# Interleaving two chunks' products and the weight product W in a fused attention and expert kernel

## Chip, cores and metric

One core of one Trainium2 chip (trn2). The metric is the device time of one execution in microseconds (us); the median of several runs is given. Engines: TensorE (PE, and PEld for its weight loads), VectorE (DVE), ScalarE (ACT), GpSimd (POOL), SyncE (SP, which issues all DMAs here).

## What is computed

Inputs: q, k, v of 4 batches x 8 heads x 576 x 64, float32; float64 weights w1, w2 (512 x 1024), w3 (1024 x 1024), w_out (1024 x 512); four experts of 512 x 1024 and 1024 x 512, float32.

```
q_s = softmax(q, over the head's 64); k_s = softmax(k, over the sequence)
x   = q_s @ (k_s.T @ v)                  per batch and head, then 2304 x 512
a, b = x @ w1, x @ w2
y   = ((a * b) @ w3) @ w_out
out = sum over experts e of p[e] * (relu(y @ e1[e]) @ e2[e]),  p = probs / sum
```

## The kernel before, in words

The tokens are cut into chunks of 512 (four, and one of 256); chunk c takes its x from the batches that hold its tokens. Every float32 product is made as three matmuls of a hi and a lo part (mm3, lines 106 to 110).

**Conversion.** w1, w2, w3 and w_out come as float64. Two 512 KB pieces make a pair (load_to, line 410). ScalarE takes the absolute value of the high words (line 123), VectorE runs four passes (lines 127 to 138), then split makes hi on ScalarE (line 102) and lo on VectorE (line 103). There are 20 pairs; the list `jobs` (384 to 386) gives their order: eight pairs of w1 and w2 slices, then pieces of w_out ("o") and of w3 ("w"). `AHEAD` loads four pairs ahead.

**Stages.** The work is written in slots, a hand-made order. Slots 6 to 13 (AB0) are ab_step(0, f): for slice f of 128 columns, a = x w1 and b = x w2 of chunk 0, 24 matmuls of 512 columns, the copy of a (479) and the product a times b (480), kept in SBUF in `prods`. The converted weights are also saved to DRAM (save_w12, 443). Slots 14 to 21 (AB1) are ab_step(1, f) with weights read back (load_w12, 448), mixed with W's units 0 to 7; slots 22 to 29 (W1) are units 8 to 15. W = w3 @ w_out is made once, 16 units of 12 matmuls (unit, 683), each block ended by a correction (454). Slots 30 to 45 are y_step for chunks 0 and 1 (h from `prods` by h_step, 486; 12 matmuls each), y stored by y_out. From slot 46 (REST) ab, h and y of chunk 2, then of chunks 3 and 4; then the experts to the end.

**Attention** of batch b is put into slots by K_SLOT, Q_SLOT and X_SLOT: k_max, k_exp, k_v (245), q_exp (266 to 288), q_norm, q_turn (313), x_stage (326, 343). Its inputs are loaded two or three slots ahead. q of batch 1, half 1 is exponentiated by ScalarE row by row (274, ON_SCALAR).

**Cooking.** From the y phase on the experts' weights are combined and split once and saved to DRAM (cooking, save_e at 608), one step a slot in the y phase, four to eight a slice later.

**Order.** A planner puts the instructions of each engine, and the DMA issues of SP, in one fixed order, from the written order as priority and its own estimate of when each is ready; so steps can move ahead of their slot. `hold(key, inst)` tells it to put an instruction behind others; it adds no wait at run time. Engines and SP's queue work in their order. `gran` tiles (4 KB a partition; x, weights, wo, w3, W, products, h) share NG = 28 slots.

Of the kernel before, what the change touches and what calls it, by code (L numbers as in the profile page):

```python
# [31 lines left out]
AB0, AB1, W1, Y0, Y1, REST = 6, 14, 22, 30, 38, 46  # L32
# [3 lines left out]
K_SLOT = [[0, 0, 0, 0], [6, 7, 8, 9], [30, 32, 34, 36], [46, 47, 48, 50]]  # L36
Q_SLOT = [[2, 2], [6, 8], [30, 34], [46, 48]]
X_SLOT = [AB0, AB1, REST, REST + 8]
# [4 lines left out]
    ("k", 1, 0): 2, ("k", 1, 1): 3, ("k", 1, 2): 4, ("k", 1, 3): 5, ("q", 1, 0): 2, ("q", 1, 1): 4,  # L43
# [7 lines left out]
ON_SCALAR = {(1, 1)}  # L51
# [3 lines left out]
def linear_attention_moe_kernel(ctx: ExitStack, tc, q, k, v, w1, w2, w3, wo, dp, e1, e2, out):  # L55
# [15 lines left out]
    NG, NR = 28, 4  # L71
# [34 lines left out]
    def mm3(ps, w_hi, w_lo, r_hi, r_lo, first, last, shared=False):  # L106
        kw = {"skip_group_check": True} if shared else {}
        nc.tensor.matmul(out=ps, lhsT=w_hi, rhs=r_hi, start=first, stop=False, **kw)  # L108
        nc.tensor.matmul(out=ps, lhsT=w_hi, rhs=r_lo, start=False, stop=False, **kw)  # L109
        nc.tensor.matmul(out=ps, lhsT=w_lo, rhs=r_hi, start=False, stop=last, **kw)  # L110
# [34 lines left out]
    class Act:  # L145
# [20 lines left out]
    def load_k(b, hp):  # L166
        t = ap_.tile([P, 2, KR + 1, D], F32, tag="kr", name="kr", bufs=4)
        src = k[b, 2 * hp:2 * hp + 2]
        nc.sync.dma_start(
            out=t[:, :, 0:KR], in_=src[:, 0:KR * P].rearrange("h (p r) d -> p h r d", p=P)  # L170
        )
        nc.sync.dma_start(out=t[0:KX, :, KR], in_=src[:, KR * P:S].rearrange("h p d -> p h d"))
        kraw[b, hp] = t

    def load_v(b, hp):
        t = ap_.tile([P, 2, KR + 1, D + 1], F32, tag="vt", name="vt", bufs=4)
        nc.gpsimd.memset(t[..., D:D + 1], 1.0)
# [142 lines left out]
    def x_stage(b, hp):  # L320
# [10 lines left out]
        for u in range(2):  # L331
            ps, a = pss[u], HALF * u
            t0 = S * b + a
            while t0 < S * b + a + HALF:
                c = t0 // CH
                n = min(chunks[c][0] + chunks[c][1], S * b + a + HALF) - t0
                i, o = t0 - S * b - a, t0 - chunks[c][0]
                hi, lo = (xa.at(c, hp, s, o, o + n) for s in range(2))
                if b > 1:
                    split(hi, lo, ps[:, i:i + n])  # L340
                else:
                    nc.scalar.activation(out=hi, in_=ps[:, i:i + n], func=ACTF.Copy)
# [5 lines left out]
                t0 += n  # L348

# [10 lines left out]
    for b in range(B):  # L360
        for j in range(2):
            s = Q_SLOT[b][j]
            if b > 0:
                put(before, s - 2, load_q, b, j)
# [4 lines left out]
        for i, hp in enumerate(PAIRS):  # L369
            s = K_SLOT[b][i]  # L370
            if b > 0:
                put(before, s - 3, load_kv, b, hp)
# [3 lines left out]
            put(after, min(s + (4 if b > 1 else 3), X_SLOT[b] - 1), x_stage, b, hp)  # L376
# [7 lines left out]
    jobs = [(x, f) for f in range(NF) for x in ("a", "b")]  # L384
    for u, (x, kt) in enumerate(UNITS):
        jobs += ([("o", kt)] if x == 0 else []) + [("w", u)]
# [5 lines left out]
    def load_to(m):  # L392
        while done["load"] < min(m, len(jobs) // 2):
# [3 lines left out]
            for i in range(2):  # L397
# [12 lines left out]
                nc.sync.dma_start(out=dst, in_=src)  # L410
# [9 lines left out]
    def b_to(m):  # L420
        while done["b"] < min(m, len(jobs) // 2):
# [23 lines left out]
    def load_w12(c, f):  # L445
        for i in range(2):
            g = gran("wg")
            gate["dma"] = [nc.sync.dma_start(out=g.bitcast(F32), in_=w12d[f, i])]
            w12.setdefault((c, f), []).append(g)
# [10 lines left out]
    hg, yps, Wg, prods, ps_z = {}, {}, {}, {}, []  # L460

    def ab_step(c, f):
# [6 lines left out]
        for i in range(2):  # L469
            ps = bank(ps_y[i] if c == 0 and f % 2 else ps_w, "ab")  # L470
            for x, kt in enumerate(PAIRS):
                o = P * kt
                mm3(
                    ps[:, 0:n], gw[i][:, 0, o:o + P], gw[i][:, 1, o:o + P],
                    xa.at(c, kt, 0), xa.at(c, kt, 1), x == 0, x == KT - 1,
                )
# [3 lines left out]
        nc.vector.tensor_tensor(out=ah, in0=pss[1][:, 0:n], in1=ah, op=ALU.mult)  # L480


    def h_step(c, f):
        n = chunks[c][1]
        h = gran("h")
        lo = split(h[:, 0, 0:n], h[:, 1, 0:n], prods[c, f // 2][:, f % 2, 0:n])[1]
        if (c, f) == (0, 3):
            gate["cook"] = [lo]
# [4 lines left out]
    def y_step(c, f):  # L493
# [11 lines left out]
        for d in range(KT):  # L505
            o = P * d
            mm3(
                yps[c, d], Wg[f][:, 0, o:o + P], Wg[f][:, 1, o:o + P],
                h[:, 0, 0:n], h[:, 1, 0:n], f == 0 and not (pair and d % 2), f == NF - 1, pair,
            )  # L510
# [13 lines left out]
    def x_free(c):  # L524
        for kk in list(xa.t):
            if kk[0] == c:
# [79 lines left out]
    def save_e(kind, n, name, g):  # L606
        ewd[kind, n, name] = d = dr.tile([P, 2, 2, 256], F32, name=f"{kind}_{n}_{name}")
        nc.sync.dma_start(out=d, in_=g.bitcast(F32))
# [3 lines left out]

    def cooking(pool):
        raws_e, waiting = {}, []
# [5 lines left out]
        def part_of(kind, n):  # L620
            def part(name, src):
                def do():
                    g = pool.tile([P, 2, 2, 256], F32R, tag="o", name="eo", bufs=NOUT)
                    for i in split(g[:, 0], g[:, 1], src):
                        hold("cook", i)
# [6 lines left out]
        for i, (kind, n) in enumerate(COOKED):  # L632
            ask(i + 1)
            for do in cook(kind, n, raws_e.pop(i), part_of(kind, n)):
                do()
                while len(waiting) > 2:
                    save_e(*waiting.pop(0))
                yield
        while waiting:
            save_e(*waiting.pop(0))  # L640
# [82 lines left out]
    for f in range(NF):  # L723
        convert(f + 2)
        slot(AB0 + f, (ab_step, 0, f))
        if f > 1:
            save_w12(f - 2)
    x_free(0)
    save_w12(NF - 2)
    save_w12(NF - 1)  # L730
    load_w12(1, 0)
    load_w12(1, 1)
    for f in range(NF):
        if f + 2 < NF:
            load_w12(1, f + 2)
        convert(8 + f + 1)
        slot(AB1 + f, (ab_step, 1, f), *([(unit, f - 1)] if f > 0 else []))
    x_free(1)
    unit(NF - 1)
    steps = [(c, f) for c in range(2) for f in range(NF)]  # L740
    for f in range(NF):
        convert(17 + f // 2)
        slot(W1 + f, (unit, 8 + f))
        if f % 2:
            h_step(*steps[f // 2])
# [7 lines left out]
    def cook_some(k):  # L753
        for _ in range(k):
            next(cooks, None)

    for i, (c, f) in enumerate(steps):
# [307 lines left out]
```

## Time and profile before

| | us |
|---|---|
| median of 3 runs | 1161.68 (1160.33 to 1163.48) |
| profiled execution | 1162.17 |
| its span | 1160.4 |
| PE / DVE / ACT / POOL busy | 1127.0 / 868.4 / 534.7 / 46.8 |

The profile is one execution. The span runs from the first to the last instruction; what lies around it is 1.8 us. Matmuls are pipelined, so that a busy PE is not PE at its peak: the time from one matmul's start to the next tells the rate.

### The profile page before, as it was taken

The page shows a single profiled execution, that of the slowest core. Times are in us where ns is not written, and L with a number is a line of the kernel's source. Part 1 is how long each engine was busy: PE and PEld are TensorE (multiplying, and loading weights), DVE is VectorE, ACT ScalarE, POOL GpSimd, SP SyncE. Part 2 cuts the span into 40 slices and gives each one's busy share as a digit, 9 for nine tenths or more (in the row PEclk, how much of TensorE's full clock was granted, in tenths as well). Part 3 has the DMA queues.
Part 4 walks back from the last instruction along what each step waited for, and adds up shares of the span by engine and source line. Part 5 has one row for each costly group of instructions (what it writes and reads, how often), then busy time and mean ns, then how long its engine had stood idle before and what let it go on. Part 6 is the DMA issues. An engine that isn't in the chain of part 4 may idle for free.

```text
span 1160.4 us, 18707 instructions
## 1 busy us (share of the span) xinstructions
PE 1127.0 (97%) x7048; PEld 1050.2 (91%) x7048; DVE 868.4 (75%) x1428; ACT 534.7 (46%) x982; POOL 46.8 (4%) x70
## 2 busy tenths in 40 slices
PE   5889999999999999999999999999999999999997
PEld 4667888787888889999999999999999999999997
DVE  7898866766457414999989987777779877777777
ACT  4665535555445315555555544433336344433441
POOL 0012300103000000000000000000000000000000
PEclk9999999999999999999999999999999999999999
DMA  9999960599799746777877888777777797777773
GB/s 238 264 352 305 372 233 1 183 381 405 282 378 356 277 164 224 288 286 283 295 275 273 287 303 307 251 251 251 250 249 257 244 305 256 248 253 249 241 262 111
DMA packets 127418, 310.12 MB, mean 267 GB/s; under 512 B 31968, under 2 KB 52960, under 8 KB 127328
## 3 DMA queue, kind: packets, MB, share of 16 engines
q1 hardware_dynamic: 126848, 308.14, 76.9%
q8 instruction: 56, 0.92, 0.3%
q10 hardware_dynamic: 480, 0.79, 0.2%
q14 instruction: 34, 0.28, 0.1%
HBM read 232.33 MB, written 76.55 MB: 266 GB/s over the span
## 4 chain that ended last, share of the span: by engine, by line
PE 86%; DVE 6%; DMA 5%; SPq 2%; issue 1%; ACT 1%; DVEq 0%; ACTq 0%
PE hp L879 28%; PE op L953 26%; PE ab L110 5%; PE ab L108 5%; PE ab L109 5%; PE y L108 3%; PE y L110 2%; PE y L109 2%; DMA kr<-in_k_dram 2%; DVE acc L937 2%; PE kv L245 2%; PE W L108 1%; PE W L109 1%; PE W L110 1%; DVE h L103 1%; DVE blk L588 1%
## 5 line engine op out<-in xcount | busy, mean ns | idle before, releaser
L953 PE MATMUL op<-eg,h 128*128 128x256 f32 x3024 | 379.9, 280 | 0.5 <-DMA eg<-e_b 0.4
L879 PE MATMUL hp<-t,eg 128*128 128x384 f32 x2016 | 377.1, 336 | 1.1 <-DVE acc L937 0.9
L953 PEld LDWEIGHTS op<-eg,h 128*128 128x128 f32 x3024 | 373.4, 188 | 1.0 <-PE hp L879 0.7
L879 PEld LDWEIGHTS hp<-t,eg 128*128 128x128 f32 x2016 | 344.6, 188 | 3.3 <-DVE acc L937 2.1
L937 DVE SCALAR_TENSOR_TENSOR acc<-op,prob,acc 128x256 f32<-128x256 f32 (+1 forms) x396 | 197.2, 527 | 43.1 <-PE op L953 43.1
L102 ACT ACTIVATE h<-blk 128x768 fp32r<-128x768 f32 x168 | 138.0, 842 | 144.5 <-DVE blk L588 108.2
L103 DVE TENSOR_TENSOR h<-blk,h 128x768 fp32r<-128x768 f32 x168 | 157.2, 950 | 24.4 <-ACT h L102 24.3
L862 ACT ACTIVATE blk<-hp 128x384 f32<-128x384 f32 x192 | 90.7, 490 | 138.8 <-PE hp L879 137.1
L866 DVE TENSOR_TENSOR blk<-hp,blk 128x384 f32<-128x384 f32 x144 | 79.3, 556 | 66.8 <-PE hp L879 63.6
L108 PE MATMUL ab<-x,wg 128*128 128x512 f32 (+1 forms) x320 | 121.1, 381 | 3.4 <-ACT wg L102 2.7
L109 PE MATMUL ab<-x,wg 128*128 128x512 f32 (+1 forms) x320 | 119.3, 373 | 0.2 <-ACT x L347 0.2
L110 PE MATMUL ab<-x,wg 128*128 128x512 f32 (+1 forms) x320 | 119.3, 375 | 0.0
L868 ACT ACTIVATE blk<-blk 128x768 f32<-128x768 f32 x72 | 60.6, 845 | 73.6 <-DVE blk L866 72.0
L588 DVE TENSOR_TENSOR blk<-blk 128x768 f32<-128x768 f32 x96 | 91.4, 952 | 0.5
L108 PEld LDWEIGHTS ab<-x,wg 128*128 128x128 f32 x320 | 60.8, 191 | 14.6 <-ACT wg L102 3.5
L109 PEld LDWEIGHTS ab<-x,wg 128*128 128x128 f32 x320 | 61.0, 191 | 10.8 <-ACT x L347 0.8
L110 PEld LDWEIGHTS ab<-x,wg 128*128 128x128 f32 x320 | 61.0, 191 | 10.8 <-DVE wg L103 0.5
L480 DVE TENSOR_TENSOR ah<-ab,ah 128x512 f32<-128x512 f32 (+1 forms) x40 | 25.4, 635 | 51.1 <-PE ab L110 46.5
L103 DVE TENSOR_TENSOR eo<-e2r,eo 128x512 fp32r<-128x512 f32 x56 | 41.6, 744 | 19.1 <-ACT eo L102 18.7
L109 PE MATMUL y<-h,W 128*128 128x512 f32 x128 | 50.3, 395 | 0.0
L110 PE MATMUL y<-h,W 128*128 128x512 f32 x128 | 49.4, 392 | 0.0
L108 PE MATMUL y<-h,W 128*128 128x512 f32 x128 | 47.9, 404 | 0.0
(98 smaller groups left out, 1037.2 us busy)
## 6 DMA issues: line engine op xcount, KB each, us to landing
eg<-e_t SPq DMA_DIRECT2D x96, 512.0 KB, 4.5
eg<-e_b SPq DMA_DIRECT2D x72, 512.0 KB, 4.8
eg<-e_s SPq DMA_DIRECT2D x68, 512.0 KB, 4.4
eg<-e_a SPq DMA_DIRECT2D x51, 512.0 KB, 4.6
wg<-w SPq DMA_DIRECT2D x48, 512.0 KB, 8.4
f<-in_moe_w_dram SPq DMA_DIRECT2D x32, 512.0 KB, 6.5
e_t<-eo SPq DMA_DIRECT2D x32, 512.0 KB, 6.3
e_s<-eg SPq DMA_DIRECT2D x28, 512.0 KB, 4.8
```

Source lines behind the costliest of these rows:

```text
L102: i = nc.scalar.activation(out=hi, in_=src, func=ACTF.Copy)
L103: j = eng.tensor_tensor(out=lo, in0=src, in1=hi.bitcast(F32), op=ALU.subtract)
L108: nc.tensor.matmul(out=ps, lhsT=w_hi, rhs=r_hi, start=first, stop=False, **kw)
L109: nc.tensor.matmul(out=ps, lhsT=w_hi, rhs=r_lo, start=False, stop=False, **kw)
L110: nc.tensor.matmul(out=ps, lhsT=w_lo, rhs=r_hi, start=False, stop=last, **kw)
L588: return lambda: nc.vector.tensor_tensor(out=dst, in0=x, in1=y, op=op)
L862: nc.scalar.activation(out=block(name)[:, u], in_=src, func=func)
L866: nc.vector.tensor_tensor(out=x[:, u], in0=src, in1=x[:, u], op=ALU.add)
L868: nc.scalar.activation(out=x, in_=x, func=ACTF.Relu)
L879: nc.tensor.matmul(out=q, lhsT=w[:, sw, kt, P * u:P * u + P], rhs=t[b][:, kt, st], start=new and kt == 0 and i == 0, stop=kt == 1 and i == ...
L937: nc.vector.scalar_tensor_tensor(out=dst, in0=src, scalar=prob[:, T, e:e + 1], in1=dst, op0=ALU.mult, op1=ALU.add,)
L953: nc.tensor.matmul(out=q[:, c:c + DH], lhsT=g[:, sh, u, P * i:P * i + P], rhs=w[:, sw, u], start=new and u == 0 and j == 0, stop=u == 1 an ...
```

## The change

Chunk 1's ab_step follows chunk 0's three slices behind (LAG) and uses the same converted weights, so that the weights are not read back for it. The order of conversion is ab pairs 0 to 4, then w_out and w3 pieces between the others; W's units start at slice 4 (WLAG 4). The products of chunks 0 and 1 are stored to DRAM and read back for h (load_ah). Batch 1's attention moves to slots 3 to 8, and its second q goes to VectorE. The part of chunk 2 that comes from batch 1 (128 tokens) is kept in one `early` tile and copied later. Loads of batches 2 and 3 are held until pair 13 is converted, those of batch 3 and of w for chunks 2 and on also behind the last matmul written ("pace"); weight loads from pair 2 on are held behind batch 1's last q load. Cooking makes two steps a slot in the y phase, held by "pace". NG is 26, and y has two buffers of its own.

```diff
-AB0, AB1, W1, Y0, Y1, REST = 6, 14, 22, 30, 38, 46
+LAG, WLAG = 3, 4
+AB0 = 6
+W1 = AB0 + 8 + LAG
+Y0 = W1 + 5
+REST = Y0 + 16
-K_SLOT = [[0, 0, 0, 0], [6, 7, 8, 9], [30, 32, 34, 36], [46, 47, 48, 50]]
-Q_SLOT = [[2, 2], [6, 8], [30, 34], [46, 48]]
-X_SLOT = [AB0, AB1, REST, REST + 8]
+K_SLOT = [
+    [0, 0, 0, 0], [3, 4, 5, 5], [Y0 - 2, Y0 - 0, Y0 - -2, Y0 + 4], [REST, REST + 1, REST + 2, REST + 4],
+]
+Q_SLOT = [[2, 2], [4, 5], [Y0 - 2, Y0], [REST, REST + 2]]
+X_SLOT = [AB0, AB0 + LAG, REST, REST + 8]
...
-ON_SCALAR = {(1, 1)}
+ON_SCALAR = set()
...
-    NG, NR = 28, 4
+    NG, NR = 26, 4
...
+            if c == 2 and b is not None and b <= P:
+                if "early" not in self.t:
+                    self.t["early"] = gran("xe")
+                return self.t["early"][:, s, P * kt + a:P * kt + b]
...
+        hold("pace" if b > 2 else ("in", b), nc.sync.dma_start(
...
+            if (b, j) == (1, 1):
+                gate["f64"] = [i]
...
+    jobs = []
+    for f in range(NF):
+        if f > WLAG:
+            jobs += [("o", f - WLAG - 1), ("w", f - WLAG - 1)]
+        jobs += [("a", f), ("b", f)]
+    for u in range(NF - WLAG - 1, len(UNITS)):
+        jobs += ([("o", u)] if u < 8 else []) + [("w", u)]
...
+                if n > 1:
+                    hold("f64", i)
...
+            if n == 13:
+                gate["in", 2] = gate["in", 3] = [last]
...
-            ps = bank(ps_y[i] if c == 0 and f % 2 else ps_w, "ab")
+            ps = bank(ps_y[i] if c == 0 and f in (1, 3) else ps_w, "ab")
...
+        if c < 2 and f % 2:
+            ahd[c, f // 2] = dr.tile([P, 2, 512], F32, name=f"ah{c}_{f // 2}")
+            nc.sync.dma_start(out=ahd[c, f // 2], in_=prods.pop((c, f // 2)))
+
+    def load_ah(c, k):
+        t = prods[c, k] = gp.tile([P, 2, 512], F32, tag="g", name="ahl")
+        nc.sync.dma_start(out=t, in_=ahd[c, k])
...
-            t = raw("yt").rearrange("p (k f) -> p k f", k=2)
+            t = gp.tile([P, 2, 512], F32, tag="y", name="yt", bufs=2)
...
-        convert(f + 2)
-        slot(AB0 + f, (ab_step, 0, f))
...
-        slot(AB1 + f, (ab_step, 1, f), *([(unit, f - 1)] if f > 0 else []))
...
+    for g in range(NF + LAG):
+        convert(g + 2 if g < WLAG else min(2 * g - 1, g + 6))
+        todo = []
+        if g < NF:
+            w12[1, g] = w12[0, g]
+            todo.append((ab_step, 0, g))
+        if g >= LAG:
+            todo.append((ab_step, 1, g - LAG))
+        if g >= WLAG:
+            todo.append((unit, g - WLAG))
+        slot(AB0 + g, *todo)
+        if 0 <= g - 2 < NF:
+            save_w12(g - 2)
...
+    load_ah(0, 0)
+    u = NF + LAG - WLAG
+    for s in range(5):
+        convert(min(20, 17 + s))
+        n = min(2, len(UNITS) - u)
+        slot(W1 + s, *[(unit, u + i) for i in range(n)])
+        u += n
+        if s > 0:
+            if s % 2:
+                load_ah(0, s // 2 + 1)
+            h_step(*steps[s - 1])
...
+            while asked < min(i + 12, len(steps)):
+                load_ah(asked // NF, asked % NF // 2)
+                asked += 2
             h_step(*steps[i + 4])
         slot(Y0 + i, (y_step, c, f))
         if i > 2:
-            cook_some(1)
+            cook_some(2)
```

## Rows read from the trace of the kernel before

**Rows 1.** The page: span, and TensorE's busy time.
```profile
span 1160.4 us, 18707 instructions
...
PE 1127.0 (97%) x7048; PEld 1050.2 (91%) x7048; DVE 868.4 (75%) x1428; ACT 534.7 (46%) x982; POOL 46.8 (4%) x70
```
**Rows 2.** Busy time by stretch: from:to, length, engines, clock, DMA share, GB/s.
```profile
20.00:210.00 190.00, 178.21 (x801) 142.20 (x801) 154.88 (x236) 104.61 (x257) 28.42 (x31) 0.98 0.79 247
33.40:50.00 16.60, 12.52 (x52) 9.11 (x53) 12.50 (x24) 9.38 (x29) 0.41 (x2) 0.90 1.03 248
50.00:80.00 30.00, 26.79 (x122) 21.20 (x121) 29.23 (x53) 20.90 (x70) 3.42 (x3) 0.94 1.08 338
80.00:120.00 40.00, 36.58 (x171) 27.79 (x169) 33.40 (x48) 24.30 (x62) 9.83 (x11) 1.00 1.01 317
120.00:217.00 97.00, 96.98 (x444) 79.78 (x443) 69.14 (x98) 44.08 (x83) 13.98 (x10) 1.00 0.54 183
217.00:265.00 48.00, 47.00 (x212) 37.88 (x212) 36.60 (x69) 30.08 (x65) 3.08 (x7) 1.00 0.91 338
250.00:260.00 10.00, 10.00 (x46) 8.20 (x45) 6.26 (x12) 4.39 (x9) 0.20 (x1) 1.00 1.03 414
```
**Rows 3.** By tile (ab, W): durations min/median/max, first and last start.
```profile
L108 PE MATMUL ab<-x,wg x320: 278/389/638, 33.4 to 438.8; 128*128 128x512 f32 x128, 128*128 128x256 f32 x32
...
L454 PEld LDWEIGHTS W<-W,nident x8: 188/191/192, 187.7 to 216.4; 128*128 128x128 f32 x8
```
**Rows 4.** Timeline of TensorE: start, duration, idle before and what ended it.
```profile
45.91 0.79 PE L216 MATMUL mt<-ident,mt 128*128 128x128 f32 x2 [3.06 <-DVE mt L214]
...
68.60 0.50 PE L108 MATMUL ab<-x,wg 128*128 128x512 f32 x1 [2.50 <-ACT wg L102]
...
70.92 0.63 PE L109 MATMUL ab<-x,wg 128*128 128x512 f32 x1
71.35 0.63 PE L110 MATMUL ab<-x,wg 128*128 128x512 f32 x1
...
127.69 0.39 PE L110 MATMUL ab<-x,wg 128*128 128x512 f32 x1
...
138.12 0.39 PE L110 MATMUL ab<-x,wg 128*128 128x512 f32 x1
```
**Rows 5.** The chain that ended last, attention's pieces: start, duration, what.
```profile
83.60 0.34 PE qt L313 x3
...
88.36 1.58 PE kv L245 x10
...
93.45 0.49 PE xp L326 x2
```
**Rows 6.** TensorE from 120 to 217 us, groups by line: y and kv.
```profile
L108 PE MATMUL y<-h,W 128*128 128x512 f32 x7 | 2.8, 418 | 0.0
...
L245 PE MATMUL kv<-vt,ek 128*128 128x130 f32 x16 | 2.1, 274 | 0.0
```
**Rows 7.** VectorE: conversion (tile f, 0 to 460 us); products and q (20 to 210).
```profile
sum 460.00, DVE 105.88 ACT 47.81; mean DVE 2.30 ACT 1.04
...
L480 DVE TENSOR_TENSOR ah<-ab,ah 128x512 f32<-128x512 f32 x16 | 11.0, 686 | 3.8 <-PE ab L110 3.7
L266 DVE TENSOR_REDUCE qm<-qr 128x18 f32<-128x1152 f32 x6 | 8.1, 1342 | 3.5 <-DMA qr<-in_q_dram 3.5
```
**Rows 8.** ScalarE's row-by-row exps of q, 0 to 420 us.
```profile
L274 ACT ACTIVATE qe<-qr,qm 128x64 f32<-128x64 f32 x18 | 6.0, 336 | 0.0
```
**Rows 9.** DMA issues, 0 to 460 us: KB each, median us to landing.
```profile
wg<-w SPq DMA_DIRECT2D x48, 512.0 KB, 8.4
...
w<-wg SPq DMA_DIRECT2D x16, 512.0 KB, 7.7
```
**Rows 10.** SP's queue at 59 us: a k load of batch 2.
```profile
59.32 0.43 SPq L169 DMA_DIRECT2D kr<-in_k_dram  x1
```
**Rows 11.** Waits of SP's queue, 0 to 460 us: total, times, longest.
```profile
SPq L608 <- DVE eo L103: 61.5, 34, 7.6
```

More of the change, by code (lines that the diff above doesn't have):

```diff
@@ L109, in mm3 @@
         nc.tensor.matmul(out=ps, lhsT=w_hi, rhs=r_lo, start=False, stop=False, **kw)
-        nc.tensor.matmul(out=ps, lhsT=w_lo, rhs=r_hi, start=False, stop=last, **kw)
+        return nc.tensor.matmul(out=ps, lhsT=w_lo, rhs=r_hi, start=False, stop=last, **kw)
     gate = {}
@@ L199, in load_q @@
             )
+            hold("pace" if b > 2 else ("in", b), i)
+            if (b, j) == (1, 1):
+                gate["f64"] = [i]
         qraw[b, j] = t
@@ L348, in x_stage @@
                 t0 += n
+        if b == 2:
+            hi = xa.at(2, hp, slice(None))
+            nc.scalar.activation(
+                out=hi[:, :, 0:P], in_=xa.t["early"][:, :, P * hp:P * hp + P].bitcast(F32),
+                func=ACTF.Copy,
+            )
     before, mid, after = {}, {}, {}
@@ L375, in linear_attention_moe_kernel @@
             put(mid, s + 2, k_v, b, hp)
[L376 to L386, printed above, removed]
+            put(after, min(s + (5 if b == 2 else 4 if b == 3 else 3), X_SLOT[b] - 1), x_stage, b, hp)
+    jobs = []
[5 more added lines that the diff above has]
+        jobs += ([("o", u)] if u < 8 else []) + [("w", u)]
     raws, ms, w3g, wog = {}, {}, {}, {}
@@ L448, in load_w12 @@
             gate["dma"] = [nc.sync.dma_start(out=g.bitcast(F32), in_=w12d[f, i])]
+            if c > 1:
+                hold("pace", gate["dma"][0])
             w12.setdefault((c, f), []).append(g)
@@ L525, in x_free @@
         for kk in list(xa.t):
-            if kk[0] == c:
+            if kk[0] == c or (c == 2 and kk == "early"):
                 del xa.t[kk]
@@ L607, in save_e, with cook_flush @@
         ewd[kind, n, name] = d = dr.tile([P, 2, 2, 256], F32, name=f"{kind}_{n}_{name}")
-        nc.sync.dma_start(out=d, in_=g.bitcast(F32))
+        return nc.sync.dma_start(out=d, in_=g.bitcast(F32))
     COOKED = [("e1", n) if i == 0 else ("e2", n) for n in range(NE1) for i in range(2)]
     COOKED += [("e2", n) for n in range(NE1, NGE)]
+    waiting = []
+    def cook_flush():
+        while len(waiting) > 2:
+            hold("pace", save_e(*waiting.pop(0)))
     def cooking(pool):
-        raws_e, waiting = {}, []
+        raws_e = {}
         def ask(i):
@@ L624, in do @@
                     for i in split(g[:, 0], g[:, 1], src):
-                        hold("cook", i)
+                        hold("pace", i)
                     waiting.append((kind, n, name, g))
@@ L634, in cooking @@
             for do in cook(kind, n, raws_e.pop(i), part_of(kind, n)):
-                do()
-                while len(waiting) > 2:
-                    save_e(*waiting.pop(0))
+                i = do()
+                if i is not None:
+                    hold("pace", i)
                 yield
         while waiting:
-            save_e(*waiting.pop(0))
+            hold("pace", save_e(*waiting.pop(0)))
     def load_y(p):
@@ L719, in linear_attention_moe_kernel @@
         slot(i)
-    for f in range(NF):
-        convert(f + 2)
-        slot(AB0 + f, (ab_step, 0, f))
[L726 to L736, printed above, removed]
-        slot(AB1 + f, (ab_step, 1, f), *([(unit, f - 1)] if f > 0 else []))
+    for g in range(NF + LAG):
[11 more added lines that the diff above has]
+            save_w12(g - 2)
+        if g == NF - 1:
+            x_free(0)
     x_free(1)
-    unit(NF - 1)
     steps = [(c, f) for c in range(2) for f in range(NF)]
[L741 to L745, printed above, removed]
+    load_ah(0, 0)
[9 more added lines that the diff above has]
+            h_step(*steps[s - 1])
     finish_lo(*prev.pop(0))
@@ L753, in cook_some @@
     def cook_some(k):
+        cook_flush()
         for _ in range(k):
             next(cooks, None)
+    asked = 6
     for i, (c, f) in enumerate(steps):
```

39 lines of the change are left out of this document (19 added, 20 removed).

## The prediction

> **What bounds the kernel now.** I read the page first, for the span and the busy shares [rows 1]: 1160.4 us, TensorE busy 97%. Busy does not say that nothing is lost, so the second view is the table by stretches [rows 2]. It shows three kinds of stretch. From 33.4 to 120 us TensorE has holes (12.5 of 16.6 us, 26.8 of 30, 36.6 of 40 busy) and a granted clock of 0.90 and 0.94 in the first two of them; VectorE is close to full there and the DMA share is at or over 1.0. From 120 to 217 us TensorE has no hole, and DMA is at 0.54. From 217 us on it is full but for 1 us. So time can only come out of the work before 120 us.
>
> The third view gives places and prices. The first ab matmul starts at 33.4 us, and the last correction of W is at 216.4 us, thus W ends at about 217 [rows 3]. In a full stretch 46 matmuls of 512 columns take 138.12 - 127.69 = 10.43 us, 0.2267 us each; after a hole the same matmul comes every 0.43 us, half the rate, the 1.2 GHz level; the holes themselves are waits for the transposed maximum of k (3.06 us) and for the hi part of a converted weight (2.50 us) [rows 4]. Each hole therefore costs its length and a slow restart.
>
> **The loss that the change can reach.** TensorE's work from 33.4 us to the end of W, without holes: ab 2 x 8 steps x 24 x 0.2267 = 87.1; W 16 x 12 x 0.2267 = 43.5 and eight corrections 1.9; batch 1's attention from [rows 5]: kv 4 x 1.4 to 1.58, xp 16 x 0.245, qt 6 groups x 0.33, small transposes and x corrections about 3, in all 14.7; what is left of batch 0 at 33.4 us about 4.2 by the same prices. Sum 151.4, so W could end at 184.8. It ends at 217, but by then TensorE has also done work of later stages: 19 y matmuls (7 + 6 + 6) and two kv rounds [rows 6], at these prices 4.3 + 3.0, with batch 2's qt (21 matmuls, 2.3), xp (1.0) and small ones (1.0) 11.6 us. W's end without them is 205.4. The loss is 205.4 - 184.8 = 20.6 us; this is the ceiling of the gain. Some 7 us of it lie before 50 us, where x of batch 0 is still being made (22 ab matmuls stand in 16.6 us): the change gives TensorE no other work there.
>
> The Trainium skill ("TensorE: Matmul & The Clock Gate", section on 56 ns against 53.3) gives 215.7 ns between matmuls of 512 columns at full clock. The trace's 226.7 ns decides; by the page the work would be some 6 us less and the ceiling about 27.
>
> **The change part by part.** *Second chunk three slices behind.* From slice 3 on each converted pair feeds 48 matmuls (10.9 us) where it fed 24 (5.44). No matmul is added or removed. This is what fills the holes after about 80 us: TensorE lost 40 - 36.6 = 3.4 us of plain idle in 80 to 120, and some 2 more by pitch, and there it now has a backlog (slices 0 to 2 of chunk 1). Between 50 and 80 us chunk 1 is not there yet: its x needs batch 1's attention, now due by slot 8 and not 13, so holes there stay unless conversions come sooner.
>
> *W mixed in from slice 4.* A unit is 12 matmuls, 2.72 us; a slice 4 to 7 then holds 13.6 us of TensorE work against two pairs of conversion. All conversions cost VectorE 105.9 us, 5.3 a pair; the sixteen products 11.0 [rows 7]: a slice costs it 10.6 + 1.4 = 12.0, less than 13.6. Over the whole stretch VectorE was busy 154.9 us from 20 to 210 us [rows 2]; some of that belongs to batches 2 and 3 (the maximum over q ran six times there at 1.34, batch 1 needs two [rows 7]), so 141 to 152 are needed before W's end. At the share of 0.87 that it reached from 33.4 to 120 us (12.5 + 29.2 + 33.4 of 86.6) the last pair is done at 20 + 147/0.87 = 189, and W 3 us later. TensorE's own earliest end with the start's 7 us is 192: the two are even.
>
> *q (1, 1) from ScalarE to VectorE.* Eighteen exps, 6.0 us with reads of the sums behind each, leave ScalarE [rows 8]; they stood ahead of the hi part for which TensorE waited 2.50 us [rows 4]. VectorE gets one subtraction and one sum, 2 x 1.34 = 2.7, counted above. I take 2 us of gain.
>
> *Loads.* Chunk 1's sixteen weight loads go, eight stores and eight loads of products of the same size come: issues even, each 512 KB and 7.7 to 8.4 us from issue to landing [rows 9], hidden by the many slices between. Inputs of batches 2 and 3, which ran as early as 59.3 us [rows 10], are held until pair 13 is converted; that relieves DMA at a share of 1.0. The early store waits for its product on SP's in-order queue, with weight loads behind it; bounded by nothing below and by one wait of SP for VectorE above, 7.6 us [rows 11]. I take zero: four pairs are loaded ahead.
>
> *Fewer slots.* 26 in place of 28. By my count slice 7 holds x 8 + 1, weights 8, wo 5, w3 2, products 2: all 26. Conversion then can't run further ahead; between 0 and one conversion's 5.3 us per refusal. I take 2 us of loss.
>
> *After W.* The y phase is 16 steps of 2.72 and batch 2, some 54 us. It gets two cooking steps a slice (about 12 MB with their raw loads), product loads 2.6 MB, batches 2 and 3 about 4.1, w 2.1, y 1.0: 22 MB, near 400 GB/s. The best 10 us of the trace moved 414, the stretch 217 to 265 on the mean 338 [rows 2]. I take it as just fitting: cooking has slack, and it is tied to the matmuls so that it does not run ahead. The four copies of the early tile and the separate y buffers are ScalarE work beside a full TensorE: zero, since ScalarE was busy 30.1 of 48 us in that phase [rows 2]; if that cover goes, 4 x 0.6.
>
> **Sum.** W's end: 184.8 + 7 (start) + 3.5 (holes left between 50 and 80: 3.2 of idle and some 2.3 of half pace there before, less 2 for q) + 2 (slots) - 2 (the start is relieved as pairs 2 and 3 are loaded later and VectorE reaches batch 0's last q sooner) = 195.3, against 205.4: a gain of 10.1. Everything behind follows, as TensorE is full from there. The profiled execution took 1162.17, its span and 1.8 around it, 0.5 over the median 1161.68; 1162.2 - 10.1 = 1152.1, **about 1151.5** against the median.
>
> **Rivals.** *VectorE or the slots set the pace.* For: 0.97 busy in 50 to 80, the full count of slots. Against: the even sum above. At a share of 0.80, 147 us end at 204 and W at 207: nothing is won. It decides from about 0.81 downwards. Time 1160.
>
> *Slower: the y phase becomes DMA-bound.* Place: the loads of the products on SP's queue behind stores of cooked weights, which waited 61.5 us in 34 times for VectorE, 7.6 at longest [rows 11]. Before, the products stood in SBUF and no such wait existed. 22 MB at 338 GB/s take 65 us where TensorE needs 54: 11 us late, and one wait of 7.6 in front: 1151.5 + 18 = 1169. It decides from an arrival more than four steps (10.9 us) late, since h is made four steps ahead. Against: loads are asked for up to twelve steps ahead.
>
> The Trainium skill ("DMA: Bandwidth & Descriptors", "Where 436 GB/s comes from") says that about 358 GB/s per core binds between HBM and SBUF. The trace's 414 GB/s speaks against it; by the page the y phase would need 61 us, 7 late, and the time would be 1158. This milder form has 0.02 of the chance of the y phase.
>
> *Nearly the whole ceiling.* The start gets shorter too, clock falls vanish: a gain of 18, 1143.5. For: both clock falls stand behind holes.
>
> *The change doesn't do what it says* would be products loaded back but W not moved: the order of the queues is made by a planner that may leave W's units where they stood; then only q's 2 us are left, 1160, counted with the first rival.
>
> **Numbers.** Forecast 0.52 (its own range 1146 to 1157), ceiling 0.13, pace or order 0.19, y phase 0.16. About 0.3%, 3.5 us, is what a measurement of this kernel can tell from no change. Faster: 0.52 + 0.13 and a third of the pace case, 0.71. Slower: 0.14 of the y phase. Same: the rest, 0.15. The range leaves out about a tenth at each side: 1142 to 1166.
>
> **What would show it.** Right: no load of w for chunk 1; W's last correction at 190 to 200 us with no y matmul ahead of it; TensorE's idle after 80 us under 1 us; granted clock 1.00 there; y's end ahead by 8 to 12 us and the experts the same length. Wrong: holes before ab of chunk 1 that end with a converted weight (pace); holes in the y phase that end with h or a product load (DMA); a span of the experts that differs.

## The result and the profile after

The changed kernel takes 1172.87 us in the median (1172.13 to 1174.02, four runs), the kernel before, beside it on the same chip, 1161.24. The ratio is 1.0101 with an interval of 1.0087 to 1.0114: 11.6 us slower, where 10 us faster was forecast. The profiled execution took 1172.86 us with a span of 1171.1. A few executions, the profiled one of e17 among them (1600 us, granted clock 0.66), took 1400 us or more and are left out of the ratios and of the table of losses below.

First the page after, for [rows 1]: TensorE's busy time has hardly changed, the span has grown by 10.7 us.

```profile
span 1171.1 us, 18660 instructions
...
PE 1129.4 (96%) x7048; PEld 1050.3 (90%) x7048; DVE 866.6 (74%) x1429; ACT 531.2 (45%) x951; POOL 46.7 (4%) x70
```

The same stretches as in [rows 2], and two more, of the kernel after (from:to, length, busy time of the engines, granted clock, DMA share, GB/s):

```profile
33.40:50.00 16.60, 13.04 (x56) 9.61 (x55) 13.57 (x20) 12.70 (x36) 0.82 (x4) 0.89 1.00 293
50.00:80.00 30.00, 27.44 (x132) 20.86 (x131) 25.72 (x44) 19.56 (x47) 0.78 (x5) 0.94 0.80 280
80.00:120.00 40.00, 38.72 (x168) 30.23 (x167) 30.39 (x40) 19.98 (x45) 0.90 (x3) 1.00 0.72 248
120.00:170.00 50.00, 49.51 (x221) 40.71 (x221) 38.34 (x53) 18.62 (x32) 5.26 (x3) 1.00 0.84 241
170.00:190.00 20.00, 16.32 (x71) 12.14 (x70) 19.84 (x24) 12.59 (x26) 3.93 (x4) 1.00 0.55 161
230.00:250.00 20.00, 16.00 (x72) 12.78 (x71) 11.27 (x30) 11.35 (x27) 10.37 (x8) 0.91 0.47 153
```

The kernel before, in the two new stretches:

```profile
170.00:190.00 20.00, 20.00 (x91) 16.50 (x90) 11.94 (x15) 9.41 (x18) 0.20 (x1) 1.00 0.16 51
230.00:250.00 20.00, 20.00 (x92) 16.36 (x91) 14.95 (x28) 11.53 (x26) 0.53 (x3) 1.00 1.02 365
```

From 80 to 120 us the holes closed, as forecast: 38.7 us busy instead of 36.6, at full clock. But two stretches in which TensorE had no hole before now lose about 4 us of busy time each: the last conversions (VectorE full, 19.84 of 20) and the end of chunk 0's y products (no engine full, DMA at less than half).

**An account of the losses.** For every kernel below I call loss what is left of a stretch when each of its matmuls is counted at its spacing where TensorE is full (0.2267 us for 512 columns [rows 4], the smaller shapes likewise). A hole and a half-rate restart both show in it; where TensorE is full it comes out below nothing (by up to 1.9 us in 50 us, by 4.0 in the longest stretch), so a negative number means no loss, and what counts is the difference between kernels. It is one execution each: the thirteen kernels whose start is that of the changed kernel lie between 32.2 and 34.9 in the first column, so a difference of less than 3 us in one stretch is not a finding by itself.

| kernel | median us | ratio to before | 0-60 | 60-120 | 120-170 | 170-220 | 220-280 | 280-460 |
|---|---|---|---|---|---|---|---|---|
| before | 1161.24 | 1 | 29.8 | 11.1 | 0.1 | -1.1 | -0.3 | -4.0 |
| after | 1172.87 | 1.0101 (1.0087-1.0114) | 34.1 | 3.8 | 0.2 | 3.7 | 7.4 | -1.8 |
| e1 | 1178.39 | 1.0128 (1.0093-1.0163) | 35.9 | 7.4 | -0.2 | 3.1 | 9.1 | -1.4 |
| e2 | 1168.50 | 1.0050 (1.0035-1.0065) | 33.6 | 12.2 | -0.6 | -1.9 | -1.6 | -0.7 |
| e3 | 1177.68 | 1.0123 (1.0086-1.0161) | 34.0 | 4.0 | 0.6 | 3.7 | 3.7 | -0.2 |
| e4 | 1166.50 | 1.0041 (1.0025-1.0056) | 34.7 | 4.9 | -0.4 | 5.3 | 0.8 | -1.5 |
| e5 | 1169.31 | 1.0065 (1.0048-1.0082) | 34.6 | 3.9 | 4.6 | -1.1 | 3.8 | -2.1 |
| e6 | 1168.21 | 1.0052 (1.0034-1.0069) | 32.2 | 4.2 | -0.8 | 1.9 | 6.4 | -1.7 |
| e7 | 1164.15 | 1.0014 (1.0002-1.0026) | 34.9 | 5.1 | 1.4 | -1.7 | 3.5 | -1.6 |
| e8 | 1178.05 | 1.0146 (1.0124-1.0168) | 31.0 | 14.0 | 0.4 | 3.4 | 11.5 | -0.9 |
| e10 | 1161.58 | 1.0000 (0.9989-1.0010) | 34.0 | 4.2 | -0.2 | -0.7 | 1.6 | -1.8 |
| e11 | 1167.33 | 1.0043 (1.0027-1.0058) | 34.7 | 4.5 | -0.8 | 0.0 | 6.8 | -2.7 |
| e12 | 1168.14 | 1.0053 (1.0033-1.0072) | 32.7 | 9.1 | -0.2 | -0.6 | 4.2 | -2.0 |
| e13 | 1162.91 | 1.0008 (0.9991-1.0024) | 34.2 | 4.2 | -0.2 | -1.1 | 3.8 | -3.3 |
| e14 | 1164.98 | 1.0025 (1.0015-1.0036) | 33.9 | 4.4 | -0.4 | -0.9 | 1.5 | 0.0 |
| e15 | 1167.94 | 1.0047 (1.0034-1.0060) | 31.1 | 9.0 | -0.4 | -1.7 | 0.9 | 0.2 |
| e16 | 1164.00 | 1.0016 (1.0005-1.0026) | 33.3 | 4.7 | 0.6 | -1.1 | 3.9 | -1.4 |
| e18 | 1166.24 | 1.0042 (1.0026-1.0059) | 32.4 | 4.5 | 1.6 | 0.6 | 2.5 | -1.8 |

Summed over the row, after stands 47.4 - 35.6 = 11.8 us behind before at 460 us, about the whole of the measured 11.6 (the two spans differ by 10.7). The change won 11.1 - 3.8 = 7.3 us between 60 and 120; the start gave back 4.3, which leaves 3.0 won by 120 us. The last conversions then lost 4.8, the end of chunk 0's products 7.7, and 2.2 went in small pieces up to 460. The experts are as long as before (the matmuls of their first product run from 442.0 to 1125.6 us before and from 452.6 to 1136.0 after). (The experiments' sums meet their spans' differences to 4 us, but for e3, which loses 5 us more after 460 us.)

**What moved.** The maximum over q (line 266 before, 281 after) marks where the attention of batches 2 and 3 runs on VectorE. In the view of one line (count, duration in ns, first and last start), from 50 us on, in the kernel before (its first is batch 1's):

```profile
L266 DVE TENSOR_REDUCE qm<-qr x5: 1332/1337/1352, 54.5 to 135.6; 128x18 f32<-128x1152 f32 x5
```

and in the kernel after:

```profile
L281 DVE TENSOR_REDUCE qm<-qr x4: 1281/1348/1353, 154.4 to 224.1; 128x18 f32<-128x1152 f32 x4
```

Before, both batches were done with this step by 137 us; their work lay in stretches that had holes anyway. After, none of it starts before 154. For batch 2 the hold on its loads until pair 13 is converted put it there. Batch 3 is not under that hold: its loads take the key "pace" alone (`hold("pace" if b > 2 else ("in", b), ...)`), so they stand behind the last matmul written, and their place goes by batch 2's slots and buffers.

**How it hurts at 170 to 190 us.** VectorE's timeline: the held load is late, and its consumer stands in VectorE's fixed order, so VectorE idles 5.3 us just ahead of the stretch in which it is full.

```profile
154.41 1.35 DVE L281 TENSOR_REDUCE qm<-qr 128x18 f32<-128x1152 f32 x1 [5.30 <-DMA qr<-in_q_dram]
...
155.88 2.37 DVE L220 TENSOR_TENSOR m<-kr 128x256 f32<-128x256 f32 x1
...
169.19 3.14 DVE L144 SCALAR_TENSOR_TENSOR f<-f,f 128x1024 int32<-128x1024 int32 x1
...
199.66 2.46 DVE L109 TENSOR_TENSOR wg<-f,wg 128x512 fp32r<-128x512 f32 x1 [0.38 <-ACT wg L108]
```

GpSimd's timeline has batch 2's own steps at the same moments (what the two engines do to each other there is told in the last section):

```profile
155.85 2.12 POOL L296 TENSOR_TENSOR qr<-qr,qm 128x1152 f32<-128x1152 f32 x1 [60.84 <-DVE qm L281]
...
168.94 2.31 POOL L296 TENSOR_TENSOR qr<-qr,qm 128x1152 f32<-128x1152 f32 x1
...
199.45 2.12 POOL L316 TENSOR_TENSOR qe<-qe,qs 128x1152 f32<-128x1152 f32 x1 [7.29 <-DVE qs L315]
```

TensorE then waits twice, for a product that frees the ab bank and for a converted weight:

```profile
174.45 0.50 PE L114 MATMUL ab<-x,wg 128*128 128x512 f32 x1 [1.96 <-DVE ah L511]
189.63 0.50 PE L116 MATMUL W<-wg 128*128 128x512 f32 x1 [1.61 <-DVE wg L109]
```

**How it hurts at 230 to 250 us.** The chain in the timeline: a GpSimd step of 5 us, the next GpSimd step behind it, an exp on ScalarE that waits for that, x's copy behind the exp in ScalarE's order, x's second half on VectorE, and TensorE's next transposed maximum behind it.

```profile
232.20 5.08 POOL L316 TENSOR_TENSOR qe<-qe,qs 128x1152 f32<-128x1152 f32 x1 [4.17 <-DVE mf L225]
...
237.28 1.67 POOL L245 TENSOR_TENSOR kr<-kr,mx 128x512 f32<-128x512 f32 x2
238.57 0.63 ACT L248 ACTIVATE ek<-kr 128x512 f32<-128x512 f32 x1 [2.09 <-POOL kr L245]
...
240.69 0.62 DVE L109 TENSOR_TENSOR x<-xp,x 128x288 fp32r<-128x288 f32 x2 [5.39 <-ACT x L108]
...
241.21 0.33 PE L227 MATMUL mt<-ident,mf 128*128 128x128 f32 x1 [3.62 <-DVE x L109]
```

The first of these steps is batch 3's, not batch 2's: the query halves pass one after the other through the one `qe` buffer, and this is the third normalization on GpSimd (batch 2's two started at 166.86 and 199.45 us). Batch 2's key step stands behind it in GpSimd's order. The granted clock of that stretch is 0.91, against 1.00 before.

**The start.** SP's queue: all of batch 1's inputs go out from 20.6 us, and weight pairs 1 to 4 only behind them.

```profile
20.57 0.53 SPq L179 DMA_DIRECT2D kr<-in_k_dram  x1
...
36.80 4.08 SPq L435 DMA_DIRECT2D f<-in_moe_w_dram  x5
```

In the kernel before, pairs 1 to 3 went out ahead of batch 1's first input, which followed at 24.96 us:

```profile
20.32 4.52 SPq L410 DMA_DIRECT2D f<-in_moe_w_dram  x6
```

The first ab matmul starts at 37.2 us instead of 33.4. But of TensorE's waits up to 60 us only one, of 1.4 us, ends with a converted weight; the others end with loads and steps of attention. How much of the 4.3 us comes from the order of the loads is not shown by this trace.

### The profile page after: what moved, and what is told of

It is laid out like the page before. It is cut to its first block, busy times and chain, and to the rows that moved or that the text cites. A ratio compares the mean times of both kernels' runs of the same rounds, so it can differ in the third digit from the quotient of the medians.

```text
span 1171.1 us, 18660 instructions
## 1 busy us (share of the span) xinstructions
PE 1129.4 (96%) x7048; PEld 1050.3 (90%) x7048; DVE 866.6 (74%) x1429; ACT 531.2 (45%) x951; POOL 46.7 (4%) x70
## 4 chain that ended last, share of the span: by engine, by line
PE 79%; DVE 9%; DMA 6%; SPq 2%; issue 2%; ACT 1%; POOL 0%; DVEq 0%; ACTq 0%; POOLq 0%
PE hp L931 29%; PE op L1005 27%; PE ab L114 4%; PE ab L116 4%; PE ab L115 4%; DMA qr<-in_q_dram 3%; PE y L114 2%; PE y L116 2%; PE y L115 2%; DVE acc L989 1%; DMA f<-in_moe_w_dram 1%; PE kv L260 1%; PE xp L341 1%; DMA ahl<-ah 1%; DVE h L109 1%
## 5 line engine op out<-in xcount | busy, mean ns | idle before, releaser
L116 PEld LDWEIGHTS ab<-x,wg 128*128 128x128 f32 x320 | 60.6, 189 | 10.1
L109 DVE TENSOR_TENSOR eo<-e2r,eo 128x512 fp32r<-128x512 f32 x56 | 38.2, 694 | 20.7 <-ACT eo L108 20.3
L115 PE MATMUL y<-h,W 128*128 128x512 f32 x128 | 50.9, 399 | 0.0
L116 PE MATMUL y<-h,W 128*128 128x512 f32 x128 | 49.7, 391 | 0.0
L510 ACT ACTIVATE ah<-ab 128x512 f32<-128x512 f32 (+1 forms) x40 | 22.1, 552 | 54.9 <-PE ab L116 54.8
```

Source lines behind the costliest of these rows:

```text
L109: j = eng.tensor_tensor(out=lo, in0=src, in1=hi.bitcast(F32), op=ALU.subtract)
L116: return nc.tensor.matmul(out=ps, lhsT=w_lo, rhs=r_hi, start=False, stop=last, **kw)
```

## The experiments

e1 to e6 and e8 are edits of the changed kernel, the others of the one named.

**e1: weight pairs 1 to 3 ahead of batch 1's inputs.**

```diff
         load_v(0, PAIRS[i])
+    load_to(4)
```

> Weight pairs 1 to 3 are asked for before batch 1's inputs, as in the kernel before; all else is the changed kernel. Theory (three separate losses: about 4 us at the start, 5 us in the last conversions, 7 us where chunk 0 of y ends): TensorE's loss up to 60 us falls from 34 to about 30 us, the other two stay, time 1169. Rival (VectorE's conversions set the end of W, so an earlier start is given back): 1172 to 1173.

Measured 1178.4, beyond both; the loss up to 60 us did not fall (35.9). Batch 1's maxima stand ahead of ab in TensorE's order, and they were now the late ones; the waits of TensorE from 20 to 50 us:

```profile
PE mt L227 <- DVE mf L225: 7.4, 1, 7.4
```

**e2: no hold at pair 13.** The edit frees batch 2 alone, since batch 3's loads stay behind "pace".

```diff
-                gate["in", 2] = gate["in", 3] = [last]
+                pass
```

> The loads of batches 2 and 3 are not held behind pair 13's conversion. Theory (batch 2's attention, held back, lands in VectorE's last conversions and at the end of chunk 0's y): both later losses shrink, 1161 to 1165, with batch 2's q and k work before 130 us. Rival (the y phase is bound by DMA or by the product loads): 1172 or more, with the same holes.

Measured 1168.5, between the two. Both late losses are gone (-1.9 and -1.6), and 60 to 120 us lose 12.2 instead of 3.8: the first of batch 2's q maxima now stands at 60.9 us, among batch 1's steps on VectorE, and a query step that TensorE needs comes late. TensorE's waits from 60 to 80 us:

```profile
PE qt L328 <- DVE qe L316: 4.9, 1, 4.9
```

So the hold wins 8.4 us at 60 to 120 us and costs 14.6 at 170 to 280.

**e3: one cooking step a slot in the y phase, as before.**

```diff
-            cook_some(2)
+            cook_some(1)
```

> One cooking step a slot in the y phase in place of two. Rival on record (y phase bound by DMA, product loads behind stores of cooked weights): the holes of 230 to 265 us go, about 1166. Theory (the hole at the end of chunk 0 is a chain GpSimd, ScalarE, VectorE of batch 2's attention): unchanged to within 1.5, 1171.5 to 1174.

Measured 1177.7, beyond both. The loss at 220 to 280 us halves, to 3.7, where the theory had it unchanged. The trace shows how: the same GpSimd step and the wait of TensorE behind it are

```profile
231.64 2.56 POOL L316 TENSOR_TENSOR qe<-qe,qs 128x1152 f32<-128x1152 f32 x1 [2.97 <-DVE mf L225]
...
239.04 0.33 PE L227 MATMUL mt<-ident,mf 128*128 128x128 f32 x1 [1.87 <-DVE x L109]
```

instead of 5.08 and 3.62 us. In the changed kernel VectorE runs five operations of cooking between 232.10 and 235.30 us, beside that step; here it runs two. So the doubled cooking has a part in the late loss, by way of GpSimd. The time got longer all the same, since the last cooked weights are missing when the experts begin; TensorE, 440 to 480 us:

```profile
PE hp L931 <- ACT eg L108: 3.5, 1, 3.5
PE hp L931 <- ACT blk L914: 2.0, 1, 2.0
```

**e4: batch 2's subtractions, maxima and query steps on VectorE instead of GpSimd.**

```diff
-ON_VECTOR = {(x, b, i) for x in "esm" for b in range(2) for i in range(4)}
+ON_VECTOR = {(x, b, i) for x in "esm" for b in range(3) for i in range(4)}
```

> Batch 2's subtractions and products of attention run on VectorE, not on GpSimd. Theory (GpSimd's slow operations stand in the chain that ends the hole at 237 to 241 us): that hole and the one at 262 go, 6 us less; VectorE gets some 9 us more, part of it beside the last conversions: 1167 to 1170. Rival (batch 2's inputs arrive too late, whoever computes): 1172 to 1175.

Measured 1166.5, just below the theory's range: 220 to 280 us lose 0.8 instead of 7.4, 170 to 220 lose 5.3 instead of 3.7.

**e5: the hold at pair 9; e6: at pair 16; e7: at pair 9, with e4's edit.**

```diff
-            if n == 13:
+            if n == 9:
```

> Batches 2 and 3's loads are held behind the conversion of pair 9 instead of pair 13. Theory (the held attention of batch 2 costs twice, 4.4 us among the last conversions and 6 to 8 us at the end of chunk 0's products, because it starts at 145 us): both losses go, and between 60 and 140 us TensorE loses 0 to 3 us more, so 1161 to 1165 us. Rival (VectorE is full all the way, so that the 14 us of batch 2's operations cost the same wherever they stand): the losses only move to an earlier stretch, 1168 to 1173 us, as with no hold at all.

Measured 1169.3. The loss of the last conversions went, half of the later one stayed (3.8), and 120 to 170 us now lose 4.6: a miss for the theory, in the rival's range.

> The loads are held behind pair 16 instead of pair 13. Theory: batch 2's operations leave the stretch of the last conversions, so the 4.4 us that TensorE loses at 170 to 190 us go, W ends at about 206 us instead of 210, and what stands at the end of chunk 0's products grows from 6 to 8 us to 10 or more: 1172 to 1177 us. Rival (the conversions alone fill VectorE): the loss at 170 to 190 us stays, and the time is 1176 us or more.

Measured 1168.2, below both. The first loss fell to 1.9, but the second did not grow (6.4). Its profiled execution is 1.9 us ahead of the changed kernel's already at 60 us, where the edit touches nothing, and the changes in the two late stretches are within what one execution can differ by. The theory had a later hold cost more; the median is 4.7 us below the changed kernel's, and what makes it so is not known.

> The hold at pair 9, and batch 2's subtractions, key maxima and query steps on VectorE instead of GpSimd. Theory: as with the hold at pair 9 alone, and the slow GpSimd chain is gone too, so the end of chunk 0's products costs nothing, against some 5 us more of VectorE before 140 us: 1160 to 1165 us. Rival (VectorE full): slower than the hold at pair 9 alone by 3 us or more.

Measured 1164.2, in the theory's range, but 3.5 us still go at 220 to 280.

**e8: batch 1 one slot later**, which puts the loads of pairs 1 to 4 ahead of batch 1's.

```diff
-    [0, 0, 0, 0], [3, 4, 5, 5], ...
+    [0, 0, 0, 0], [4, 5, 6, 6], ...
-Q_SLOT = [[2, 2], [4, 5], ...
+Q_SLOT = [[2, 2], [5, 6], ...
```

> Batch 1's attention is planned one slot later (keys at 4, 5, 6, 6, queries at 5, 6), which puts the loads of weight pairs 1 to 4 ahead of batch 1's loads on SP's queue. Theory (the start loses 4 us because pairs 1 to 4 are asked for at 36.8 us and batch 1's maxima stand ahead of the first ab): the loss up to 60 us goes from 34 to 30 us, the rest as it was, 1168 to 1170 us. Rival (batch 1's x comes late at chunk 1's first ab, which needs it three slices on): the loss comes back at 60 to 80 us, 1172 to 1176 us.

Measured 1178.1, beyond both. The start recovers 3.1 us (31.0), as the theory had it, 60 to 120 us lose 10 more, as the rival had it, and 220 to 280 us lose 4 more, which neither had. TensorE's waits from 50 to 80 us are for batch 1's steps and for converted weights:

```profile
PE ab L116 <- DVE wg L109: 3.6, 2, 2.0
PE qt L328 <- DVE qe L316: 2.3, 1, 2.3
PE mt L231 <- DVE mt L229: 1.9, 1, 1.9
```

**e10: e7, and batch 2's attention three slots earlier.**

```diff
-    [Y0 - 2, Y0 - 0, Y0 - -2, Y0 + 4]
+    [Y0 - 5, Y0 - 4, Y0 - 2, Y0 - 1]
-    [Y0 - 2, Y0]
+    [Y0 - 4, Y0 - 2]
```

> As the hold at pair 9 with batch 2 on VectorE (1164.2 us), and batch 2's attention planned three slots earlier (keys at Y0-5, -4, -2, -1, queries at Y0-4, -2). Theory (what still costs 4 us at 230 to 260 us is the last pair of batch 2, which stands in the slots at the end of chunk 0's products): that loss goes, and 120 to 200 us lose 0 to 2 us more: 1160 to 1163 us. Rival (VectorE full before W's end): the loss moves into 120 to 200 us, 1164 to 1168 us.

Measured 1161.6, ratio 1.0000: the whole of the 11.6 us is back, and no more. (Batch 3's loads are placed by batch 2's slots, so they come earlier too.) What this kernel wins against the kernel before at 60 to 120 us (6.9) it loses again at the start (4.2) and after 220 us (4.1). The first late loss is gone, and of the second 1.6 us are left (the windows of 230 to 250 and of 170 to 190 us, columns as above):

```profile
230.00:250.00 20.00, 18.75 (x83) 14.56 (x83) 13.96 (x31) 13.76 (x33) 2.67 (x4) 1.00 0.82 261
170.00:190.00 20.00, 20.00 (x93) 16.38 (x92) 19.25 (x26) 13.94 (x26) 2.44 (x1) 1.00 0.70 211
```

and the q maxima run earlier than in the changed kernel:

```profile
L281 DVE TENSOR_REDUCE qm<-qr x4: 1334/1350/1353, 136.8 to 193.7; 128x18 f32<-128x1152 f32 x4
```

**e11: e7 with the hold at pair 16.**

```diff
-            if n == 9:
+            if n == 16:
```

> Hold at pair 16, batch 2 on VectorE. Theory (the stretch of the last conversions is spared by the late hold, the end of chunk 0's products by the quicker engine): 1162 to 1165 us, with the loss at 170 to 200 us at 2 us or less and that at 230 to 260 us at 2 to 4 us. Rival (the operations put on VectorE land on the last conversions, as with the hold at 13): loss at 170 to 200 us of 5 us or more and 1165 to 1168 us.

Measured 1167.3, in the rival's range but not by its mechanism: 170 to 220 us lose nothing, 220 to 280 lose 6.8. With batch 2 on VectorE, a later hold moves the loss into the y phase (0.8 with the hold at 13 in e4, 6.8 here); with batch 2 on GpSimd, e6 did not show it.

**e12: e7 with pair 1's load ahead of batch 1's; e15: e14 with it between batch 1's loads.**

```diff
-            load_to(1)
+            load_to(2)
```

in e12, and in e15

```diff
     for i in range(AB0):
+        if i == 2:
+            load_to(2)
```

> As the hold at pair 9 with batch 2 on VectorE, and weight pair 1 loaded with pair 0, ahead of batch 1's loads. Theory (part of the start's loss of 5 us against the kernel before is pair 1 asked for at 36.8 us): the loss up to 60 us falls by 2 to 3 us, 1161 to 1162.5 us. Rival (batch 1's loads, 2 to 3 us later, delay batch 1's maxima, which stand ahead of ab in TensorE's order): loss to 80 us the same or larger by up to 3 us, 1164 to 1167 us.

Measured 1168.1. The start is 2.2 us better than e7's, within what like starts differ by, and 60 to 120 us lose 4.0 more: the rival's case, 1.1 us beyond its range.

> As that kernel, and weight pair 1 loaded between the first and the second half of batch 1's loads. Theory (the start's loss is the price of batch 1's attention, whose loads and maxima come before the first ab whichever way the loads are ordered): the loss up to 80 us is the same within 1.5 us or larger, 1159 to 1164 us. Rival (it is the order of the loads): the loss up to 60 us falls by 2 to 4 us and stays so at 80 us, 1155 to 1158 us.

Measured 1167.9, beyond both. Up to 60 us the loss falls by 2.8, by 120 us it is 1.8 above e14's: TensorE waited 4.8 us there for batch 1's query step, as in e2. No order of these loads that was tried wins back the start's loss without losing as much or more by 120 us.

**e13: e7, and e14: e10, with no cooking before chunk 1's products.**

```diff
-        if i > 2:
-            cook_some(2)
+        if i > 8:
+            cook_some(4)
```

> As the hold at pair 9 with batch 2 on VectorE, but none of the expert weights' cooking until chunk 1's products have begun (then four parts a slot instead of two). Theory (at 220 to 240 us VectorE is 18 of 20 us busy, half of it with cooking, and batch 2's x waits behind that): the loss at 230 to 260 us falls from 4 us to 1 us or less, 1161 to 1162 us. Rival (what is late there is the chain of batch 2's attention itself, through ScalarE, and not VectorE's load): the loss stays at 3 us or more, and the time at 1164 us or above, since the cooking then ends later.

> Hold at pair 9, batch 2 on VectorE and three slots earlier (1161.6 us), and no cooking until chunk 1's products have begun. Theory (what the early slots leave at 220 to 240 us, 2.8 us, is batch 2's x behind the cooking on VectorE): 1158 to 1160.5 us, below the kernel before. Rival (the 2.8 us are the attention's own chain): 1161 to 1163 us.

Measured 1162.9, between the two ranges, and 1165.0, beyond both. The loss at 220 to 280 us stays (3.8 against 3.5, 1.5 against 1.6), which is the rival's case both times: with batch 2 on VectorE, cooking is not what is late there. Why e14 is 3.4 us slower than e10 is not known; 1.8 us of it stands at 280 to 460 us, where the cooking now falls, and that is within what one execution can differ by.

**e16: e10 with batch 2 left on GpSimd** (e4's edit undone).

> Hold at pair 9 and the early slots, batch 2 left on GpSimd. Theory (the place of batch 2's attention decides, the engine lengthens its chain): the loss at 220 to 270 us is 2 to 5 us against 8 in the changed kernel, 1163 to 1167 us. Rival (GpSimd's slow chain alone makes the loss): 6 us or more lost at 220 to 270 us, 1168 to 1170 us.

Measured 1164.0, 3.9 us lost at 220 to 280, as the theory had it. Taken in this order, the 11.3 us from the changed kernel to e10 divide as 3.6 for the hold at pair 9 (e5), 5.3 for the earlier slots (e16), and 2.4 for VectorE in GpSimd's stead (e10). Taken in another order they divide otherwise: 6.4 for VectorE (e4), 2.3 for the hold (e7), 2.6 for the slots (e10). The three edits reach the same loss from different sides, so the runs do not say which of place and engine decides more. Each pair of edits that was tried brings most of it (8.7 us in e7, 8.9 in e16), a single one less (3.6 and 6.4).

**e17: e10 with batch 1's second query step on ScalarE again; e18: e10 with the hold at pair 11.**

```diff
-ON_SCALAR = set()
+ON_SCALAR = {(1, 1)}
```

in e17, and in e18

```diff
-            if n == 9:
+            if n == 11:
```

> The kernel with the hold at pair 9 and batch 2 early on VectorE (1161.6 us), with the second query step of batch 1 on ScalarE again, as in the kernel before. Theory (VectorE is what is late at 50 to 60 us, and this takes some 4 us of subtraction and sum from it): the loss up to 60 us falls by 2 to 4 us, 1157.5 to 1160 us. Rival (ScalarE, which makes the first halves of the converted weights and x, has no room there: its 18 small operations stand ahead of those): the loss up to 80 us is the same or larger, 1161.5 to 1166 us.

Measured 1168.9 (ratio 1.0056, 1.0040 to 1.0073): the rival's direction, beyond its range. The one trace kept of it is of the execution left out of the table. In it the 18 small operations fill ScalarE from 66.4 to 72.3 us, and TensorE waits 6.3 us for the query step behind them, where it waits 0.5 us in e10. That would account for the 7 us by which e17 is slower than e10, but no trace of an execution of that length shows it.

> As the kernel with the hold at pair 9 and batch 2 early on VectorE, held at pair 11. Theory (with early slots the place is set by the slots, and the hold only shifts the loads by some 12 us): 1161 to 1164 us, with 0 to 2 us of loss at 150 to 200 us. Rival (the later loads put the operations on the last conversions again): 3 us or more lost at 150 to 200 us, 1164 to 1168 us.

Measured 1166.2, in the rival's range, but with less lost among the conversions than it had: 1.6 us at 120 to 170 and 0.6 at 170 to 220 are lost, 2.5 at 220 to 280. The hold's pair still matters by some microseconds.

No version beats the kernel before; e10 equals it, and e13 (0.9991 to 1.0024) can't be told from it.

## Why the prediction was wrong

**The bound was right, the main gain only in part.** The time was to be had before 120 us. From 80 to 120 us the holes closed as forecast, loads of w for chunk 1 are gone, and TensorE is full at full clock from 100 to 150 us. But from 50 to 80 us little changed: 3.2 us of idle before and 2.6 after, at a clock of 0.94 both times. By 120 us the net gain is 3.0 us, where the sum had 10.1. Nor is the 7.3 us won at 60 to 120 the interleave's alone: without the hold (e2) that stretch loses 12.2, more than the 11.1 before.

**The step that failed is "Everything behind follows, as TensorE is full from there".** The 11.6 us of TensorE's later work that the sum took out of W's end before were, apart from the 19 y matmuls, attention of batch 2. That attention had its own VectorE, ScalarE and GpSimd steps, and the sum counted these only as VectorE time that W's end no longer needs ("141 to 152"); behind W it gave them no cost. Held back, they still had to be done, between 154 us and chunk 2, and there they are a chain through three engines with fixed orders, not a sum of busy times. It cost 4.8 us among the last conversions and 7.7 at the end of chunk 0's products. This is shown: taking the hold away removes both (e2), and moving this work earlier and off GpSimd removes the first and most of the second (1.6 left of 7.4) without the price of e2 (e10). In the second the doubled cooking has a part, which the prediction weighed only in bytes: halved, it leaves 3.7 (e3).

**The start, 7 us unchanged and 2 us relieved**, was wrong in sign: the start lost 4.3 more. The prediction took the later loads of the weight pairs for a relief of 2 us and gave the earlier attention of batch 1 no wait there; pairs 1 to 4 are asked for at 36.8 us, and the first ab starts 3.8 us later. Which of the two makes the 4.3 us stays open: each other order of the loads that was tried cost as much or more later (e1, e8, e12, e15). Whether a larger lag would help was not tried.

**The last pair done at 189, and W 3 us later**: VectorE's busy time from 20 to 210 us is 151.2, inside the range of 141 to 152, but it was not at a share of 0.87. From 33.4 to 120 us it is at (13.57 + 25.72 + 30.39)/86.6 = 0.80, and from 80 to 170 us at (30.39 + 38.34)/90 = 0.76, where TensorE has 88.2 us of 90 busy and sets the pace. The last pair's fourth pass starts at 197.7 us and W's last correction at 215.4, hardly before the 216.4 of [rows 3] and with 18 y matmuls ahead of it, as in the kernel before, where the prediction had none. A share taken where VectorE was the bound does not hold where it is not.

**q (1, 1), 2 us of gain,** has the right side: put back on ScalarE in e10, it costs some 7 us (e17). **Slots, 2 us of loss**: no wait that points to it was found. **Product loads, zero,** holds: no hole of TensorE in the y phase ends with h or a loaded product. SP's wait for a product before its store was longer than the bound of 7.6 us; SP's waits up to 460 us (total, times, longest) have it at 12.9, and no wait of TensorE shows it:

```profile
SPq L514 <- DVE ah L511: 20.2, 5, 12.9
```

Whether it delayed a weight load behind it was not tried.

**The rivals.** VectorE as the pace came true in one stretch: from 170 to 190 us it is 19.84 of 20 us busy, and the two waits of TensorE shown there are for it. But the conversions alone do not fill it, since the loss goes with the hold (e2), and the share of 0.80, at which that rival had W end late and the time at 1160, makes only part of what was measured. The slower rival had the stretch and the side, not the mechanism: DMA is at 0.47 and 153 GB/s where TensorE waits, and cooking acts there through VectorE and GpSimd (e3). "The planner leaves the order" is not what happened either: it kept to the new order, holds included. That the late loss is a chain of attention through the in-order queues was on no list.

## What to carry to other kernels

Before work is held back to relieve a stretch, ask where it will run instead, and lay its whole chain, engine by engine, over that stretch; here the attention of batches 2 and 3 ran in stretches that had holes anyway, and the same work, moved beside a full TensorE, made holes of its own. When a change fills the holes, whatever else lived in them needs a new place, which has to be chosen with the change, not left to a hold. A wait at the head of an in-order queue costs also what stands behind it (5.3 us of VectorE at 149 us), so a late load belongs late in the order of its consumer.

## What was not expected of the hardware

VectorE and GpSimd held each other up here. The three VectorE operations shown above began 0.03 to 0.25 us after a GpSimd operation and took 2.37, 3.14 and 2.46 us, where the same ones take 0.41, 1.22 and 0.68 alone: 1.8 to 2.0 us more, beside GpSimd operations of 2.12 to 2.31. At 232.20 us it was GpSimd's turn, 5.08 us instead of 2.12, beside five operations of cooking on VectorE; beside two of them (e3) the same step took 2.56. The Trainium skill ("SBUF — State Buffer", section "Who interferes with whom") says that VectorE and GpSimd share one pair of ports under an exclusive lock, that a VectorE instruction with two inputs in SBUF contends for it, and that the one that comes later is blocked outright; the trace agrees, with these numbers, and all three VectorE operations have two such inputs.
